# Linear attention and an eight-expert MoE on one core: q transposed before its feature map, k^T v and num in the same PSUM banks, loads and front order rewritten

## The chip, the cores and the metric

The kernel runs on one NeuronCore of a Trainium2 chip. A core has a matrix engine (TensorE, PE in the profile), a vector engine (VectorE, DVE), an activation engine (ScalarE, ACT), a general engine (GpSimd, POOL) and a synchronisation engine (SyncE, SP). Each of them takes its instructions strictly in the order in which they were written, and they wait for each other through semaphores. Matmul results land in PSUM, which has eight banks of 2 KB per partition; everything else lies in SBUF. Loads from memory are issued by POOL (which converts fp32 to fp16 on the way) or by SP, and run on 16 shared DMA engines. The metric is device time in microseconds of one execution; lower is better.

## The reference, cut to what matters

```python
def _attn_ref(q, k, v):                       # [8, 8, 576, 64] each
    def phi(x):
        return np.where(x > 0, x, np.exp(x) - 1.0) + 1.0
    q_p, k_p = (phi(q), phi(k))
    kv = np.einsum('bhsd,bhse->bhde', k_p, v)
    z = np.sum(k_p, axis=2)
    num = np.einsum('bhsd,bhde->bhse', q_p, kv)
    den = np.einsum('bhsd,bhd->bhs', q_p, z)[..., None] + 1e-06
    return num / den

def _moe_ref(x, w_gate, w1, w2):              # x [4608, 512], w1 [8, 512, 1024], w2 [8, 1024, 512]
    P = np.exp(logits - logits.max())         # logits = x @ w_gate, then 8 rounds of row and column scaling
    for e in range(E):
        out += P[:, e:e + 1] * (np.maximum(x @ w1[e], 0.0) @ w2[e])
```

The attention output, with its heads side by side, is the x of the MoE: 4608 tokens of 512 features. The feature map phi is computed as min(max(x + 1, 1), exp(x)).

## The kernel before

**Attention in units.** A unit is one batch and four heads; there are 16, in order. For each unit the kernel loads k, q and v (`att`, L385). k stays fp32; q is converted to fp16 by the load for all units but the first, and lies in three slots of the tile `hb`; v has three tiles `vv0` to `vv2`, with a third plane of ones that gives z beside kv. The load of k for unit 0 and of q for unit 0 are issued by SP, all others by POOL.

From k: ACT takes exp (`ek`, L417), DVE takes max(k + 1, 1) (`t`, L421) and the min of both (L425). PE multiplies this with v in 36 small matmuls (`kv_ps`, L446, 64 by 64 tiles), and ACT or DVE copies the 256 columns to SBUF (`kvz`, L359 or L361).

From q: ACT takes exp (`eq`, L477) and DVE takes max (`tq`, L480), both out of SBUF; DVE takes their min (L484); PE transposes the result in 36 steps into the two PSUM banks of the tile `att` (L469); DVE (for the last two units ACT) copies it to SBUF (`qpT`, L361 or L359).

Then, for each half c of the unit's tokens: PE computes den into the two banks of `att` (L504), ACT takes Ln of it (L516); after both halves ACT takes exp(-Ln) over both (`rden`, L521), which is 1/den; PE computes num (`num_ps`, L504), and DVE multiplies the two into `xT` (L531). `kv_ps` and `num_ps` are the same two banks, used in turn (the pool `p_kv` of one).

**MoE.** Tokens are taken in nine groups of 512. For expert 0, layer 1 (`hq`, L717) of a group follows as soon as its x is there, ACT or DVE applies the relu into `hb`, and layer 2 (`ye`, L1017) follows. For the later expert 0 groups and for experts 1 to 7, the two layers are computed with seven products of half blocks in place of eight (L832, L1133), which runs PE without a break from about 120 us to the end. The routing weights are computed on DVE with one small matmul per round (L589) meanwhile.

**Weights.** w1 of expert 0 comes in two halves of 512 columns, w2 of expert 0 in two halves of four row blocks; the first matmuls of layer 1 need the first half of w1, the others the second.

**What sets the order.** Every step is a task of a small planner (`_Plan`): it has an engine, a cost, dependences and the buffers it takes and frees. `run` goes through the tasks and writes out each one's instructions. For the first 2192 tasks, which cover the front up to about 190 us, the order is not chosen but read from a table of task numbers and engines, `_FRONT` (p PE, a ACT, d DVE, g POOL, s SP, m DMA, n none). So each engine's order in the front is fixed by this table, and an instruction that has to wait holds up everything behind it on its engine. A framework below adds the semaphore waits between engines when the instructions are written out. Until the first layer 1 matmuls, 46 dummy matmuls (`yw`, L621) keep PE running.

Of the kernel before, what the change touches and what calls it, by code (L numbers as in the profile page):

```python
# [141 lines left out]
1n 2p 3p 4p 5p 48s 49m 6p 7p 8p 0g 9p 10p 11p 12p 13p 14p 15p 16p 17p 18p 19p 20p 21p  # L142
22p 23p 54a 50s 51m 60n 61a 114g 115m 120a 24p 25p 55d 56d 62d 63d 26p 27p 52g 53m 64p 65d 57n 58p
121d 59a 28p 29p 75g 76m 77g 78m 82d 122d 30p 31p 66p 32p 33p 79g 80m 34p 116g 117m 35p 36p 37p 38p
39p 81a 87n 83d 89d 84n 67a 68p 40p 88a 90d 69a 70a 41p 85p 86d 91p 92d 42p 43p 73p 93p 44p 45p
74d 71p 126n 128d 104n 127a 118g 119m 94a 105g 106m 72d 46p 95p 96a 47p 129d 97a 123n 109n 124p 125d 130p 143g
144m 153n 579n 154a 131d 98p 99d 580p 141g 142m 581p 132p 133a 147a 100p 101d 582p 583p 584p 586p 588p 587a 148d 155d
585a 590p 107g 108m 145g 146m 134p 135a 589d 156d 149d 150n 592p 593a 594p 136a 170g 171m 180n 151p 152a 110g 111m 112g
113m 157p 158d 596p 139p 591a 140d 182d 159p 595a 160a 181a 598p 183d 168g 169m 172g 173m 137p 138d 161p 162a 597a 599a
197g 198m 195g 196m 175d 600p 602p 184p 185d 603p 610a 174a 176d 207n 616n 177n 601p 608a 163a 606p 607p 199g 200m 224g  # L150
225m 226g 227m 178p 179a 186p 187a 166p 167d 201a 208a 604p 236n 164p 209d 165d 202d 203d 210d 204n 188p 605p 617p 618a
619p 620d 621p 189a 190a 622a 211p 238d 253g 254m 212d 205p 230a 206a 228g 229m 251g 252m 280g 281m 102g 103m 282g 283m
231d 623p 625p 624d 626d 213p 193p 194d 237a 239d 232d 214a 627p 614a 628a 629p 215p 216a 217a 191p 192d 631p 649n 632a
233n 612d 240p 241d 234p 235a 255g 256m 637p 218p 242p 243a 635p 244p 630d 258d 257a 245a 219d 220p 259d 260n 284g 285m
263n 265d 221d 292n 334g 335m 293a 264a 287d 638p 636p 222p 643a 223a 650p 651a 652p 266d 645d 267p 246a 653a 311g 312m
309g 310m 307g 308m 261p 268d 314d 262d 286a 654p 656p 657a 655d 294d 319n 336g 337m 633p 269p 295d 249p 250d 658p 660p
659d 288d 321d 320a 270a 313a 639p 661a 247p 271p 272a 273a 315d 248d 662p 289n 340a 663a 296p 297d 290p 291d 322d 640p
361g 362m 338g 339m 274p 298p 275d 299a 365g 366m 634p 535d 300p 301a 276p 277d 367a 664p 536d 665d 316n 682n 317p 323p
318a 647a 302a 341d 363g 364m 392g 393m 390g 391m 542d 368d 324d 683p 684a 685p 342d 686a 346n 348d 347a 668p 278p 279a
373n 374a 543d 375d 687p 688a 303p 444g 445m 325p 326a 369d 537d 304d 689p 453s 376d 544d 349d 690a 641a 669p 305p 327p  # L160
328a 329a 691p 306d 343n 350p 692d 351d 344p 345a 446g 447m 454s 476g 477m 402n 396a 666p 330p 394g 395m 417g 418m 352p
353a 448g 449m 455s 404d 667p 397d 354p 403a 355a 331d 332p 474g 475m 483s 674a 356a 484s 370n 693p 333d 371p 372d 377p
378d 459n 405d 478g 479m 485s 419g 420m 695p 359p 379p 694a 538s 539m 360d 676d 398d 424d 461d 696a 380a 423a 460a 670p
671p 672p 357p 381p 382a 673p 697p 486g 358d 425d 462d 480a 406p 407d 698d 715n 399n 400p 429n 383a 680a 401a 481d 716p
717a 421g 422m 386p 408p 409a 545s 546m 431d 387d 718p 720p 719a 563d 564d 565d 566s 567m 430a 432d 410p 411a 384p 385d
678a 426n 482d 705p 547s 548m 706p 713a 721a 412a 433p 434d 427p 428d 549d 722p 435p 413p 724p 414d 436a 723a 550d 725d
437p 438a 439a 415p 416d 726p 463p 464a 556d 440p 557d 551d 540s 541m 490n 491a 552s 553m 492d 441d 451d 493d 558d 559s
560m 570g 554s 555m 487n 571n 572g 573m 574g 575m 701p 702p 388p 488p 450a 452d 389a 489a 494p 442p 443d 728p 709d 729d
456n 457p 495a 496p 497a 458d 703p 498p 499a 500a 501p 704p 727d 465p 466a 502d 711d 730p 731a 734p 467p 468a 469a 503p
504d 759d 760d 735p 742a 699p 472p 473d 700p 470p 471d 533n 755d 748d 981s 982m 983s 984m 749d 808d 750d 756d 561s 562m  # L170
707a 751s 752m 985s 986m 987s 988m 757d 758d 753s 754m 738p 739p 732p 763n 733p 534p 809d 810d 761d 811s 812m 813s 814m
989s 990m 991s 992m 505p 506a 740a 508d 507n 576n 577g 578m 764p 778p 765a 766p 767a 780p 781a 770p 771a 768p 769a 772p
736p 774p 993s 994m 779a 784p 785a 782p 783a 746a 773d 775d 509p 510d 786p 787d 788p 789d 776p 737p 973d 815n 777a 816p
817a 511d 790p 791a 818p 819a 822p 820p 744d 762d 821a 823a 830p 832p 833a 831a 824p 825d 794p 826p 866d 867d 827d 834p
836p 837a 838p 795p 840p 974d 868d 839d 869s 870m 828p 829a 512p 835a 841d 513d 802d 792p 793p 874p 875a 800a 876p 877a
1023s 1024m 1025s 1026m 568s 569m 1027s 1028m 842p 880p 798p 514d 924d 878p 843a 844d 881a 975d 925d 845d 926d 846d 515p 796p
799p 797p 804a 871s 872m 927s 928m 516d 929s 930m 873n 884p 882p 885d 883d 888p 848p 517d 879a 889a 894p 976d 886p 895a
849a 890p 891a 806a 898p 892p 893a 847d 899d 854p 887a 896p 518p 850p 851a 855a 519d 520d 897d 852p 900p 932p 901a 853a
858p 859d 856p 857d 946p 933a 938p 902d 903d 904d 939a 521p 934p 522d 860p 935a 861a 936p 942p 906p 948p 931n 937a 943d
947a 944p 952p 949a 940p 953a 523d 941d 908p 954p 955d 945a 950p 956p 907a 951a 995p 996a 909a 957d 524p 525d 526d 997p  # L180
958p 998a 1001p 1002a 912p 1003p 1004d 999p 1005p 1006d 959a 913a 916p 917d 910p 527p 905d 528d 529d 1007p 1009p 1011p 1000a 1010a
1012a 918p 1015p 1016a 1008a 1017p 1013p 1014a 1018d 1019p 919a 530p 531d 532d 712a 1020d 1037p 914p 1039p 1038a 613a 972n 1029s 1030m
1031s 1032m 1033s 1034m 1035s 1036m 1485n 1040a 977d 915d 960p 1021p 1043p 1119s 1120m 1121s 1122m 1123s 1124m 1486g 1487m 1488g 1489m 961p
968d 978d 1044a 1022a 1093d 962p 963p 969a 964p 864a 1045p 966p 1094d 979d 1041p 1095d 1046d 1042a 609a 1047p 611d 681a 965p 1048d
1049p 675d 1051p 1053p 648a 1052a 615d 980d 1054a 1050a 967p 1057p 1058a 1059p 1055p 1061p 1065p 1067p 1096d 971d 1062d 1060d 970d 1063p
1056a 1066a 1071p 1068a 911d 1073p 1069p 1097p 1099p 1100d 679d 1064a 1072a 1101d 1098a 1102p 1103a 1075p 1107p 1110p 1076d 1077p 1079p 1108d
1070a 743d 1111d 1109d 646a 1081p 1113p 1078a 1080a 1085p 1125s 1126m 1127s 1128m 1082a 1087p 1086a 1105a 714a 1104g 1106g 1129s 1130m 1083p
1074d 1089p 1133p 1135p 1084a 1114d 1112d 1088d 1115d 1116p 1090d 1091p 1131s 1132m 1241s 1242m 1243s 1244m 1245s 1246m 1490n 1491g 1492m 1134a
1139p 1136a 642a 1092a 1141p 1140a 1137p 1118d 1117d 1161d 1162d 1165p 1167p 1166a 1170p 1143p 1175p 1138a 644a 1163d 1164d 1169d 710d 1168d
1173a 1174g 1171a 1144d 1178p 1145p 1146a 1147p 1177d 1176d 708d 1172g 1148a 1149p 1150a 1181p 1153p 1179d 1142d 1154a 1155p 1151p 1157p 1183d  # L190
1180d 1182d 1158d 1187p 677a 1189p 1184p 1159p 1215d 1216d 1186d 747d 1185d 1217d 741d 1218d 1152a 1188a 1193p 801a 1190a 1195p 1191p 1219p
1221p 1194a 1222d 1196d 1223d 1192a 1220a 1224p 1227a 1228g 923a 1160a 1197p 1198d 1156d 1229p 1231d 1232p 1230d 1493d 865d 1233d 1199p 1200a
1201p 1202a 1203p 1204a 803a 1235p 1207p 1209p 1247s 1248m 1205p 1208a 1211p 1225a 1236d 1494d 1495d 1237d 1249s 1250m 1251s 1252m 1253s 1254m
1255p 1363s 1364m 1365s 1366m 1257p 1238p 1212d 1206a 1256a 1210d 1213p 1261p 1258a 1263p 1259p 1367s 1368m 1214a 807a 1240d 1234d 1239d 1287p
1262a 1288a 1283d 1289p 1292p 1284d 1285d 1293a 1291d 1290d 1286d 1265p 1297p 1300p 745d 1266d 1267p 1260a 1299d 1302d 1298d 1301d 1269p 1271p
1303p 1268a 1270a 1275p 1264d 1272a 1277p 1273p 1304d 1337d 1305d 1276a 1279p 1309p 1311p 1306p 1338d 1274a 1226g 1280d 1281p 1295a 1310a 863a
# [41 lines left out]
def kernel(  # L238
# [17 lines left out]
    P = 128  # L256
# [65 lines left out]
    p_ye = [S_.pool(1) for _ in range(4)]  # L322
    p_sw = S_.pool(8)

    def load_w(ten, nm, pl, pieces, e, prio, deps=(), shape=None):
        g = S_.grp(pl)
        ts_ = []

# [1020 lines left out]
```

## Time and profile before

| | |
|---|---|
| median of 3 runs | 951.25 us (950.62 to 951.71) |
| the profiled execution | 951.94 us |
| its span, first instruction to last | 950.1 us |
| PE busy | 939.9 us, 99% of the span |
| of this, the 46 dummy matmuls | 14.1 us |
| DVE, ACT, POOL busy | 765.3, 575.8, 144.3 us |
| granted TensorE clock | 1.00 in every stage |

The span is what the profiler saw of the program on the core; the execution's own time is 1.84 us more. A line of a timeline gives the start in us, the time to the end of the last of its instructions, the engine, the source line, the operation with its output and inputs, a count, and in brackets the idle time before it with what ended it. PE's matmuls overlap at their ends, so a block of four 512-column matmuls shows as 1.03 us and takes 0.865 of PE's time. Stages (answers by window) give each engine's busy time within that stretch.

### The profile page before, as it was taken

Reading aid. Unit: us, or ns where it says so; the run is one execution under the profiler, and the core shown is the slowest. Engines: PE = TensorE matmul, PEld = TensorE weight load, DVE = VectorE, ACT = ScalarE, POOL = GpSimd, SP = SyncE. Lnnn points to the kernel's source line nnn. Section 1 sums busy time; section 2 is a strip of 40 time slices with the busy share of each in tenths; the row PEclk is TensorE's granted clock in tenths of the full one; section 3 lists DMA queues with packets and bytes.
Section 4 is the critical chain, followed back from the end, with each engine's and each line's share of the span. In section 5 each row is a group of like instructions: output and inputs, shape, how many; then the busy total and the mean of one; then the engine's idle time right before and its main releaser. Section 6 shows DMA issues by size and latency. Waiting matters only on the chain.

```text
span 950.1 us, 19908 instructions
## 1 busy us (share of the span) xinstructions
PE 939.9 (99%) x7816; PEld 631.7 (66%) x7816; DVE 765.3 (81%) x1479; ACT 575.8 (61%) x1025; POOL 144.3 (15%) x204
## 2 busy tenths in 40 slices
PE   9999999999999999999999999999999999999997
PEld 4444478666676666766677666766667666776665
DVE  7699899879877888788887888878887888877776
ACT  6899856666655555555555555555555555555552
POOL 5433100011111111110011111111112111111110
PEclk9999999999999999999999999999999999999999
DMA  9989793452254222652236222652226422215544
GB/s 239 265 185 235 170 230 94 122 122 78 79 126 86 75 77 78 162 122 78 79 87 119 79 78 78 152 114 70 68 67 143 111 78 78 73 45 166 167 134 134
DMA packets 82042, 112.75 MB, mean 119 GB/s; under 512 B 7324, under 2 KB 46236, under 8 KB 81948
## 3 DMA queue, kind: packets, MB, share of 16 engines
q1 hardware_dynamic: 56876, 75.59, 26.0%
q0 software_dynamic: 24320, 34.78, 19.6%
q8 instruction: 61, 1.00, 0.4%
q10 hardware_dynamic: 752, 1.11, 0.3%
q14 instruction: 33, 0.27, 0.1%
HBM read 119.69 MB, written 17.69 MB: 145 GB/s over the span
## 4 chain that ended last, share of the span: by engine, by line
PE 94%; DMA 4%; ACT 1%; DVE 1%; POOL 0%; issue 0%
PE ye L1133 35%; PE hq L832 24%; PE R L832 12%; PE Zye L832 6%; PE Zye L1133 6%; PE ye L1017 5%; PE hq L717 3%; DMA w<-in_moe_w_dram 2%; DMA vv<-in_v_dram 2%; PE kv_ps L446 1%; PE att L504 0%; PE num_ps L504 0%; PE hq L1229 0%; DMA kin<-in_k_dram 0%; PE att L469 0%; PE R L1229 0%
## 5 line engine op out<-in xcount | busy, mean ns | idle before, releaser
L1164 DVE SCALAR_TENSOR_TENSOR acc<-ye,P_sb,acc 128x256 f32<-128x256 f32 x620 | 268.4, 479 | 126.9 <-PE ye L1133 126.2
L1133 PEld LDWEIGHTS <-S 128*128 128x128 f16 x1984 | 194.0, 98 | 46.6 <-DVE S L1104 0.2
L1133 PE MATMUL ye<-T,S 128*128 128x256 f16 x1488 | 192.8, 273 | 0.0
L1174 POOL TENSOR_TENSOR acc<-acc,st 128x256 f32<-128x256 f32 x124 | 88.1, 730 | 635.2 <-ACT st L1171 624.0
L832 PEld LDWEIGHTS <-W 128*128 128x128 f16 x1248 | 122.1, 98 | 86.6
L1133 PEld LDWEIGHTS <-hb 128*128 128x128 f16 x1536 | 150.3, 98 | 42.5 <-issue 1.3
L863 ACT ACTIVATE hb<-hq 128x512 f16<-128x512 f32 x134 | 80.2, 598 | 136.6 <-PE hq L832 130.2
L832 PE MATMUL R<-xs,W 128*128 128x512 f16 (+1 forms) x560 | 150.0, 358 | 0.0
L832 PE MATMUL hq<-xs,W 128*128 128x512 f16 (+1 forms) x560 | 150.0, 358 | 0.0
L832 PE MATMUL hq<-xs,w 128*128 128x512 f16 (+1 forms) x560 | 139.7, 358 | 0.0
L832 PEld LDWEIGHTS <-w 128*128 128x128 f16 x936 | 91.5, 98 | 59.8 <-issue 0.5
L860 ACT ACTIVATE hb<-Zye 128x512 f16<-128x512 f32 x134 | 80.1, 598 | 38.5 <-PE Zye L832 38.3
L1171 ACT ACTIVATE st<-Zye,P_sb 128x256 f32<-128x256 f32 x124 | 52.5, 471 | 77.2 <-PE Zye L1133 77.0
L866 DVE CUSTOM_DVE_ANT_0 hb<-hq,sx 128x512 f16<-128x512 f32 x126 | 86.6, 687 | 15.0 <-PE hq L832 14.9
L853 ACT COPY sx<-hq 128x512 f32<-128x512 f32 x126 | 73.6, 584 | 35.3 <-PE hq L832 35.3
L849 ACT COPY Zye<-hq 128x512 f32<-128x512 f32 x134 | 77.9, 581 | 22.6 <-PE hq L832 22.4
L866 DVE CUSTOM_DVE_ANT_0 hb<-R,sx 128x512 f16<-128x512 f32 x126 | 86.5, 687 | 4.9 <-ACT sx L853 3.8
L1104 DVE TENSOR_TENSOR S<-hb 128x1024 f16<-128x1024 f16 x124 | 85.0, 686 | 5.0 <-ACT hb L863 5.0
L832 PE MATMUL Zye<-xs,w 128*128 128x512 f16 (+1 forms) x280 | 75.0, 358 | 0.0
L857 ACT COPY sx<-R 128x512 f32<-128x512 f32 x126 | 74.4, 591 | 0.0
L1133 PE MATMUL ye<-w,hb 128*128 128x256 f16 x512 | 66.3, 273 | 0.6 <-DVE acc L1164 0.5
L1133 PE MATMUL Zye<-w,hb 128*128 128x256 f16 x512 | 66.3, 273 | 0.0
(119 smaller groups left out, 940.8 us busy)
## 6 DMA issues: line engine op xcount, KB each, us to landing
xs<-xd SPq DMA_DIRECT2D x196, 256.0 KB, 3.3
w<-in_moe_w_dram POOLq DMA_DIRECT2D x18, 512.0 KB, 7.7
kin<-in_k_dram POOLq DMA_DIRECT2D x15, 576.0 KB, 7.4
out_dram<-acc SPq DMA_DIRECT2D x61, 128.0 KB, 2.4
w<-in_moe_w_dram POOLq DMA_DIRECT2D x7, 1024.0 KB, 9.8
xs<-xd SPq DMA_DIRECT2D x49, 128.0 KB, 3.2
vv<-in_v_dram POOLq DMA_DIRECT2D x16, 288.0 KB, 7.2
hb<-in_q_dram POOLq DMA_DIRECT2D x15, 288.0 KB, 6.4
```

The source lines that it names most:

```text
L832: nc.tensor.matmul(dst_[:, p, :] if parts == 2 else dst_.rearrange("p a b -> p (a b)"), lhsT=lhs(p, c), rhs=blk[i](c), start=(first and p ...
L849: nc.scalar.copy(out=Zt[1], in_=gX["tile"])
L853: nc.scalar.copy(out=gs2["tile"], in_=gX["tile"])
L857: nc.scalar.copy(out=gs5["tile"], in_=gR["tile"])
L860: nc.scalar.activation(out=dst(0, 0), in_=Zt[1], func=AF.Relu)
L863: nc.scalar.activation(out=dst(1, 0), in_=gX["tile"], func=AF.Relu)
L866: nc.vector._custom_dve(TENSOR_ADD_SAT, out=out_, in0=ps, in1=sb, s0=3.0e38, s1=0.0)
L1104: nc.vector.tensor_tensor(out=Sx[:, i], in0=a0, in1=a1, op=op)
L1133: nc.tensor.matmul(bank(g_)[:, s, :], lhsT=lhs(s, kk), rhs=rhs(kk), start=(new and s == 0 and kk == 0), stop=(kk == 3), skip_group_check=True)
L1164: nc.vector.scalar_tensor_tensor(out=dst(), in0=bank(g_)[:, s, :], scalar=P_sb[:, gg, e:e + 1], in1=dst(), op0=ALU.mult, op1=ALU.add)
L1171: nc.scalar.mul(out=gst["tile"], in_=bank(g_)[:, s, :], mul=P_sb[:, gg, e:e + 1])
L1174: nc.gpsimd.tensor_tensor(out=dst(), in0=dst(), in1=gst["tile"], op=ALU.add)
```

## The change

1. **q is transposed as loaded** (units 1 to 15). PE transposes the raw fp16 q into PSUM; ACT's exp and DVE's max then both read the transposed q from PSUM and write SBUF, and DVE's min gives `qpT` there. The copy out of PSUM is gone, and so is the tile `tq` but for unit 0, which goes as before. Unit 1 uses the banks of `ye0` and `ye1` in place of `att`, with exp and max in halves.
2. **k^T v beside num.** One tile `kvn` of two banks is taken once. num uses its columns 0 to 287, kv its columns 384 to 511; the planner has a pool for each, where one served both.
3. **Loads.** w1 of expert 0 comes in three pieces, of 256, 256 and 512 columns; all loads are made to follow the first of their queue, and their order on POOL is new: v0, k1, q1, v1, w1 (two pieces), q2, k2, v2, w1 (last), k3, q3, v3, w2 (two pieces), and so on, where it was k1, v0, k2, q1, v1, q2, v2, w1, q3, k3, w1, v3, q4, w2, w2.
4. **exp(-Ln) in halves** for the first two units.
5. **38 dummy matmuls** in place of 46, new costs in the planner, and a **new table** `_FRONT`.

```diff
-    p_kv = S_.pool(1)
+    p_kv, p_num = S_.pool(1), S_.pool(1)
+    kvn = kvps.tile([P, 2, 512], FP32, tag="kv", name="kvn")
...
-            gkv["tile"] = kvps.tile([P, 2, 512], FP32, tag="kv", name="kv_ps")
+            gkv["tile"] = kvn[:, :, 384:384 + 2 * D]
...
-            return load_w(moe_w1, "w1", p_w1, [[((slice(None), slice(None), slice(512 * i, 512 * i + 512)),
-                                                 512 * i, [[F, P], [P * F, NDT], [1, 512]])] for i in range(2)], e, shape=[P, NDT, F], **kw)
+            return load_w(moe_w1, "w1", p_w1, [[((slice(None), slice(None), slice(a, a + n)),
+                                                 a, [[F, P], [P * F, NDT], [1, n]])] for a, n in ((0, 256), (256, 256), (512, 512))],
+                          e, shape=[P, NDT, F], costs=(0.0013 * 1024, 0.0013 * 1024, 2.65), **kw)
...
-                        nc.tensor.transpose(qps()[half(r), hh, j, :], gtq["tile"][half(hh), j, r, :],
+                        nc.tensor.transpose(qin(hh)[half(r), j, :],
+                                            gtq["tile"][half(hh), j, r, :] if n == 0 else gin["q"]["tile"][half(hh), r, j, :],
                                             ident[half(hh), half(hh)])
...
+            t1 = fadd(("pe", 0.29), f_qt, deps=[tin["q"], t_id[0]], acq=ga, use=[gin["q"]], prio=pr, cfg=1)
+            t0 = fadd(("none", 0.0), f_qa, deps=[t1], acq=[geq], prio=pr)
+            ta = fadd(("none", 0.0), f_gq, deps=[t1], acq=[gq], prio=pr)
+            te2 = []
+            for hs in range(2 if n == 1 else 1):
+                def f_qe(_, hs=hs):
+                    o, i = qio(geq["tile"], hs)
+                    nc.scalar.activation(out=o, in_=i, func=AF.Exp)
+
+                def f_qm(_, hs=hs):
+                    o, i = qio(gq["tile"], hs)
+                    nc.vector.tensor_scalar(out=o, in0=i, scalar1=1.0, scalar2=1.0, op0=ALU.add, op1=ALU.max)
+                us = [ga[hs]] if n == 1 else ga
+                te2.append(fadd(("act", 0.65 if n == 1 else 1.16), f_qe, deps=[t0], use=[*us, geq], prio=pr))
+                te2.append(fadd(("dve", 0.44 if n == 1 else 0.76 if b < NR else 1.36), f_qm, deps=[ta], use=[*us, gq], prio=pr))
+
+            def f_qp(_):
+                nc.vector.tensor_tensor(out=gq["tile"], in0=gq["tile"], in1=geq["tile"].rearrange("p r j d -> p r (j d)"), op=ALU.min)
+            tq = fadd(("dve", 0.76), f_qp, deps=te2, use=[geq, gq], prio=pr)
...
-            gn = S_.grp(p_kv)
+            gn = S_.grp(p_num)
...
-                gn["tile"] = kvps.tile([P, 2, 512], FP32, tag="kv", name="num_ps")
+                gn["tile"] = kvn[:, :, 0:CH]
...
-    for i in range(46):
-        twa = add(("pe", 0.43 if i < 9 else 0.215), f_warm, deps=[twa], use=[gyw], prio=900.0, after=1.2 + 0.25 * i)
+    for i in range(38):
+        twa = add(("pe", 0.43 if i < 14 else 0.215), f_warm, deps=[twa], use=[gyw], prio=900.0, after=1.2 + 0.25 * i)
...
-            t1 = add(("pe", 0.2175 * (c1 - c0)), f_hq, deps=[tw1[0 if g == 0 and f < 4 else 1], prev_hq[0]] + xd_[0:c1 if g == 0 else None],
+            t1 = add(("pe", 0.2175 * (c1 - c0)), f_hq, deps=[tw1[f // 2 if g == 0 and f < 4 else -1], prev_hq[0]] + xd_[0:c1 if g == 0 else None],
```

Here n is the unit, b its batch, `qin` and `qio` give the PSUM view of the transposed q (for unit 1 one bank per half), and `p r j d` are partition, head pair, token block and feature.

More of the change, by code (lines that the diff above doesn't have):

```diff
@@ L323, with load_w @@
     p_sw = S_.pool(8)
-    def load_w(ten, nm, pl, pieces, e, prio, deps=(), shape=None):
+    def load_w(ten, nm, pl, pieces, e, prio, deps=(), shape=None, costs=None):
         g = S_.grp(pl)
@@ L445, in f_kv @@
                     for r in range(2):
-                        nc.tensor.matmul(gkv["tile"][half(r), hh, 0:2 * D].rearrange("p (z d) -> p z d", z=2),
+                        nc.tensor.matmul(gkv["tile"][half(r), hh, :].rearrange("p (z d) -> p z d", z=2),
                                          lhsT=gt["tile"][half(hh), j, r, :], rhs=gin["v"]["tile"][half(hh), r:r + 2, j, :],
@@ L456, in f_z, with qin @@
         def f_z(e):
-            copy(e, gz["tile"], gkv["tile"][:, :, 0:2 * D].rearrange("p h (z d) -> p h z d", z=2))
+            copy(e, gz["tile"], gkv["tile"].rearrange("p h (z d) -> p h z d", z=2))
         tz = [fadd({"dve": 0.43, "act": 0.37}, f_z, deps=[tkv], use=[gkv, gz], prio=pr)]
         gq, geq = S_.grp(p_qpT), S_.grp(p_eq)
-        ga = [S_.grp(p_att), S_.grp(p_att)]
+        ga = [S_.grp(p_ye[0]), S_.grp(p_ye[1])] if n == 1 else [S_.grp(p_att), S_.grp(p_att)]
         def qps():
             return at2.bitcast(FP16)[:, :, 0:S].rearrange("p h (j w) -> p h j w", w=PW)
+        def qin(hh):
+            if n == 1:
+                return ga[hh]["tile"].bitcast(FP16)[:, 0:S].rearrange("p (j w) -> p j w", w=PW)
+            return qps()[:, hh]
         def f_qt(_):
+            for hh in range(2 if n == 1 else 0):
+                ga[hh]["tile"] = yps.tile([P, 512], FP32, tag=f"ye{hh}", name=f"ye{hh}")
             for j in range(NJ):
@@ L473, in f_qa @@
             geq["tile"] = fp.tile([P, 2, NJ, D], FP16, tag="ek", name="eq", bufs=3)
-            gtq["tile"] = fp.tile([P, NJ, 2, D], FP16, tag="tq", name="tq")
-        def f_qe(_):
-            nc.scalar.activation(out=geq["tile"], in_=gin["q"]["tile"], func=AF.Exp)
-        def f_qm(_):
-            nc.vector.tensor_scalar(out=gtq["tile"].rearrange("p j r d -> p r j d"), in0=gin["q"]["tile"], scalar1=1.0, scalar2=1.0, op0=ALU.add, op1=ALU.max)
-        def f_qp(_):
-            tv = gtq["tile"].rearrange("p j r d -> p r j d")
-            nc.vector.tensor_tensor(out=tv, in0=tv, in1=geq["tile"], op=ALU.min)
@@ L486, in f_qc, with f_gq, qio @@
-        def f_qc(e):
+            if n == 0:
+                gtq["tile"] = fp.tile([P, NJ, 2, D], FP16, tag="tq", name="tq", bufs=1)
+        def f_gq(_):
             gq["tile"] = fp.tile([P, 2, S], FP16, tag="qpT", name="qpT")
+        def qio(t, hs):
+            dst = t.rearrange("p r j d -> p r (j d)") if len(t.shape) == 4 else t
+            if n == 1:
+                return dst[:, hs], qin(hs).rearrange("p j w -> p (j w)")
             if b >= NR:
-                copy(e, gq["tile"].rearrange("p h (w j) -> p h w j", j=NJ), qps().rearrange("p h j w -> p h w j"))
-            else:
-                copy(e, gq["tile"], at2.bitcast(FP16)[:, :, 0:S])
@@ L492, in att @@
[L492 to L498 removed]
+                return dst.rearrange("p h (w j) -> p h w j", j=NJ), qps().rearrange("p h j w -> p h w j")
@@ L499, in att @@
+        tqs = [tq]
         grd = S_.grp(p_rden)
@@ L521, in f_ex, with f_exh @@
             nc.scalar.activation(out=grd["tile"], in_=grd["tile"], func=AF.Exp, scale=-1.0)
-        te_ = fadd(("act", 1.18), f_ex, deps=tl, use=[grd], prio=pr)
+        te_ = []
         for c in range(2):
-            gn = S_.grp(p_kv)
+            def f_exh(_, c=c):
+                nc.scalar.activation(out=grd["tile"][:, c], in_=grd["tile"][:, c], func=AF.Exp, scale=-1.0)
+            if n < 2:
+                te_.append(fadd(("act", 0.62), f_exh, deps=[tl[c]], use=[grd], prio=pr))
+            elif c == 0:
+                te_ = [fadd(("act", 1.18), f_ex, deps=tl, use=[grd], prio=pr)] * 2
+        for c in range(2):
+            gn = S_.grp(p_num)
             def f_num(_, c=c, gn=gn):
-                gn["tile"] = kvps.tile([P, 2, 512], FP32, tag="kv", name="num_ps")
+                gn["tile"] = kvn[:, :, 0:CH]
                 heads(gn["tile"], c, 0)
@@ L636 @@
     gsw = S_.grp(p_sw)
-    ti = add(("pool", 0.8), f_wg, acq=[gsw], use=[gsw], prio=-96.5, after=1.75)
+    ti = add(("pool", 0.8), f_wg, acq=[gsw], use=[gsw], prio=-96.5, after=1.75, deps=[first_ld["pool"]])
     wg_done.append(add(("dma", 0.3), lambda _: None, deps=[ti], use=[gsw], prio=-96.5, lat=2.15))
```

233 lines of the change are left out of this document (125 added, 108 removed).

## The prediction

> **What bounds the kernel now.** First the page's busy times and slices, then the table of 10 us stages, then PE's timeline where a stage is not full, last one unit of attention followed over three engines.
>
> ```profile
> PE 939.9 (99%) x7816; PEld 631.7 (66%) x7816; DVE 765.3 (81%) x1479; ACT 575.8 (61%) x1025; POOL 144.3 (15%) x204
> DMA  9989793452254222652236222652226422215544
> ```
>
> TensorE is the bound; DMA is full only in the first 100 us.
>
> ```profile
> 10.00:20.00 10.00, 9.40 (x260) 4.80 (x253) 8.51 (x14) 7.86 (x10) 5.79 (x8) 1.00 1.18 197
> 20.00:30.00 10.00, 9.28 (x149) 4.12 (x138) 6.55 (x11) 8.32 (x13) 4.32 (x6) 1.00 1.20 235
> 30.00:40.00 10.00, 8.84 (x120) 3.95 (x118) 5.11 (x8) 7.66 (x12) 2.87 (x4) 1.00 1.16 282
> 90.00:100.00 10.00, 9.03 (x178) 4.20 (x173) 9.50 (x17) 9.41 (x15) 1.50 (x2) 1.00 0.86 205
> 100.00:110.00 10.00, 9.68 (x240) 5.20 (x233) 9.19 (x19) 8.25 (x11) 0.00 (x0) 1.00 0.56 162
> ```
>
> The columns are stage, length, and busy us of PE, PEld, DVE, ACT, POOL. Every other stage from 40 to 190 is full, and from 200 to the end PE lacks 5.1 us, mostly the tail. So the end moves by what PE gains or loses before about 125 us, where attention ends.
>
> ```profile
> 20.60 1.04 PE L717 MATMUL hq<-xT,w 128*128 128x512 f16 x4
> 25.66 1.90 PE L717 MATMUL hq<-xT,w 128*128 128x512 f16 x8 [0.56 <-DMA w<-in_moe_w_dram]
> 34.09 3.61 PE L1017 MATMUL ye<-w,hb 128*128 128x512 f16 x16 [0.68 <-DMA w<-in_moe_w_dram]
> 38.82 0.32 PE L504 MATMUL att<-qpT,kvz 64*64 64x288 f16 x4 [0.48 <-ACT kvz L359]
> 99.75 0.47 PE L446 MATMUL kv_ps<-vv,t 64*64 64x128 f16 x18 [0.97 <-DMA vv<-in_v_dram]
> 108.29 0.48 PE L469 MATMUL att<-ident,tq 64*64 64x64 f16 x36 [0.32 <-ACT P_sb L552]
> ```
>
> The first useful layer-1 matmul is at 20.60. Twice PE then waits for expert 0's weights; after 34.09 it loses only 0.48 + 0.97 + 0.32 = 1.77 us.
>
> ```profile
> 40.06 0.45 DVE L480 TENSOR_SCALAR tq<-hb 128x1152 f16<-128x1152 f16 x1
> 40.88 1.15 ACT L477 ACTIVATE eq<-hb 128x1152 f16<-128x1152 f16 x1
> 44.12 0.48 PE L469 MATMUL att<-ident,tq 64*64 64x64 f16 x36
> 44.73 0.76 DVE L361 COPY qpT<-att 128x1152 f16<-128x1152 f16 x1
> 46.87 0.32 PE L504 MATMUL att<-qpT,kvz 64*64 64x288 f16 x4
> ```
>
> One unit's q: max and exp read SBUF and need not wait for each other, min follows, and only then PE transposes; the banks "att" have one reader, the 0.76 us copy.
>
> **Method.** I laid the changed kernel's built order out in time, instruction by instruction: each instruction starts at the later of its engine's previous end and the end of what it waits for (plus 0.2 after PE, 0.05 after ACT or DVE), with durations from the rows above and their like (min 0.75, x product 0.76, Ln 0.73, exp 1.16, kvz copy 0.37 on ACT, ye or hq block of four 0.865, kv 0.53, PE turn between 64- and 128-row tiles 0.13). The old order so laid out puts the first hq at 20.2 (trace 20.6), the wait at 38.4 at 0.62 (trace 0.48) and the end at 949.1 (span 950.1).
>
> **Loads (a gain).** POOL's old queue stood until 6.12 for the first k buffer; the new one issues v0, k1, q1, v1, both 256-column pieces of w1 and q2 before the load that needs it. v0 takes k1's place and lands at about 8.2 (k1: 1.46 + 6.7). On SP nothing moves. The gate copy on POOL now stands ahead of v14 and the last four q: the layout has the last v land 0.7 before its kv, so 0; at worst the 0.97 of the old 99.75 comes back. Ahead of the second w2 piece stands one q load less: -1.45 (w1's first half landed at 20.2, the q behind it at 21.65). The 256-column rows make 512-byte packets, which no load here has: by bytes alone the two cost what the one did (+0), by packets alone twice 2.5 instead of 2.5 (+2.5). Single cast packets took 98 ns at 1024 bytes, 107 at 1152 and 172 at 2048; their line gives 61 at 512, so +0.65, which I take. With 0.3 for the earlier start, w2's second piece lands at about 33.0 instead of 34.1: **-1.1**. The first hq comes out at 16.8, 3.8 earlier, but that is not the gain: PE runs into w2. Eight warm matmuls fewer cost nothing, since the rest only fill PE before 16.8. For the first two units exp is cut in halves, not seen here: 0.58 (half of 1.16) to 0.73 (Ln of 576), I take 0.66; hidden behind w2.
>
> **Old waits.** The 1.77 us after 34.09 belonged to the old order; I count them as gone: **-1.8** (bounds 0 and -1.8).
>
> **Engine work.** Fifteen copies go (13 x 0.76 DVE, 2 x 1.1 ACT). max, 0.45 on fp16 in SBUF, now reads fp16 in PSUM. Not in this trace; the nearest row is the copy of the same 1152 elements from the same bank, 0.76, which I take; bounds 0.45, and 1.45 if it runs at the fp32 PSUM pace (0.76 for 576). exp from PSUM stays 1.16 (ACT's copy of the bank took 1.10). Six kvz copies go from DVE to ACT, 0.37 each. All of this lies beside PE; alone it moves nothing.
>
> **New waits (loss).** The built order of the changed kernel (line numbers of its own) shows what each instruction waits for. Two engines that read or write one PSUM tile's bank now wait for each other, even in different columns:
>
> ```
> L531 Activation eq_940<-att_78 128x1152 [waits DVE_49,PE_49]
> L535 TensorScalarPtr qpT_941<-att_78 128x1152 [waits Activation_49]
> L362 TensorCopy kvz0_103<-kvn_108 128x256 [waits DVE_49]
> ```
>
> Here max (L535) waits for the exp of the same q in 11 of the 14 units 2 to 15, in units 7, 9 and 15 exp waits for max; the copy of kv (L362) waits for an x product reading num in other columns, x products wait for kv copies, and kv's matmuls wait for x products. The planner's tasks name none of these as dependences, so its fixed order puts nothing there to cover them. From transposes to den: 0.2 + 1.16 + 0.05 + 0.76 + 0.75 = 2.9 us, where side by side it would be 2.1. And DVE is a queue: while max waits, x products behind it wait, and PE's second num waits for them.
>
> Unit 5: transposes end 46.5; exp 46.7 to 47.9; max 47.9 to 48.65; x of unit 4 behind it 48.6 to 49.35; num, which needs its bank, at 49.4. PE has only a 0.87 block, to 48.17, and the turn: 1.1 idle.
> Unit 13: transposes end 104.1; the kv copy must also wait for num in its bank, exp 105.8 to 107.0, max to 107.8, two queued DVE steps, min 109.1 to 109.8, den 109.8. PE is done at 108.0: 1.7 idle.
> Unit 15: kv waits for unit 14's x, behind max: 1.4 idle at 122.3; then the kvz copy behind exp and that x: 1.4 at 127.2.
>
> All waits after the second w2 piece, in order from 38 us: 0.71, 1.11, 0.77, 0.50, 0.87, 0.44, 0.35, 0.57, 0.50, 0.56, 1.09, 0.13, 0.51, 1.66, 0.24, 0.50, 1.39, 1.42: **+13.3**. Before w2 they cost nothing, as w2 is later (den of unit 3 is ready at 30.5, w2's first piece at 30.4). No filler can come forward: the order is a fixed list. In the same layout the waits of "att" alone come to 10.9, those of the kv and num banks alone to 4.7; they overlap.
>
> **Sum.** -1.1 - 1.8 + 13.3 = +10.4 on a span of 950.1 gives 960.5; with the 1.84 us around it (951.94 - 950.1) 962.3. The profiled execution stood 0.7 above the median of 951.25, so the median becomes **961.7**.
>
> **The rule weighed.** The Trainium skill, "PSUM — Partial Sum Buffer", section "PSUM bank collisions raise a hardware error", says that no two engines may be in one bank at a time, reads against reads included, and that they must be kept apart by bank. By that rule the waits cannot be dropped and the sum stays 961.7; without them it would be 948.4. No run here shows a collision. On max's price, "VectorE: DVE Perf Modes", section "Why PSUM operands drop a tier", caps an operand in PSUM one step below what SBUF allows; that speaks for 0.76 against 0.45 (959.0 by 0.45).
>
> **Rivals.**
> 1. Faster: the bank waits fall under PE's blocks, because Ln, exp and kv copies land otherwise than laid out. Then -1.1 - 1.8 = -2.9: 948.4. For it: old PE had 100% in 40 to 90 with DVE at 85 to 100%. Against: a block is 0.87 and the chain 2.9, and DVE's queue passes each delay on. It decides where the 18 waits sum to under 2.9 us.
> 2. max from PSUM costs 1.45: each of 14 chains is 0.69 longer; laid out so, the end comes 7.9 later: 969.6. For it: fp32 from PSUM runs at that pace; against: the fp16 copy's 0.76.
> 3. Half of the waits are absorbed (max at 0.45, PE turns shorter): +6.6 - 2.9 = +3.7: 955.
> 4. The 512-byte packets cost the full 2.5: w2 at 34.9, +1.9 on the sum: 963.6.
>
> **Chances.** Forecast 0.66 with rival 4 inside it (957 to 966), rival 2 0.12, rival 3 0.14, rival 1 0.05, within 0.2% 0.03. 0.2% (1.9 us) is about what a measurement can tell. Faster 0.05, same 0.03, slower 0.92. The range leaves out rival 1, half of rival 2 and some of rival 3: 956 to 969.
>
> **What will show it.** After: first hq near 16.8; w2's second piece near 33; from 38 to 128 us a dozen or more PE waits of 0.4 to 1.7, put down to DVE xT, DVE qpT and ACT kvz; DVE's max starting where ACT's eq of the same unit ends; max 0.76 long; from 200 us on no difference but the offset. Wrong if the PE stages from 40 to 130 stay full, or max and exp of one unit overlap.

## The result: 1.5% slower, and the profile after

The changed kernel takes 965.65 us (median of 4 runs, 965.26 to 966.16), the kernel before 951.10 (4 runs, 950.62 to 951.71). The ratio is 1.0153, with a 95% interval of 1.0135 to 1.0171. The profiled execution took 965.41 us with a span of 963.6, 13.5 more than the 950.1 of before.

The page of the changed kernel, the lines that answer to those of before:

```profile
PE 938.9 (97%) x7808; PEld 632.7 (66%) x7808; DVE 765.1 (79%) x1469; ACT 574.4 (60%) x1024; POOL 145.3 (15%) x205
PE   8888889999999999999999999999999999999997
DMA  9978586435226322542226422442226522215544
```

PE is busy as long as before, but for 97% of the span and not 99%: the time is added as idle PE, and the six slices with an 8 say that it lies in the first 145 us.

The stages of the changed kernel (stage, length, then busy us of PE, PEld, DVE, ACT and POOL, the granted clock, DMA's share, GB/s):

```profile
10.00:20.00 10.00, 9.36 (x169) 4.39 (x168) 7.45 (x12) 9.43 (x14) 5.61 (x7) 1.00 1.26 234
20.00:30.00 10.00, 7.16 (x144) 3.52 (x143) 6.92 (x11) 7.52 (x11) 3.67 (x5) 1.00 1.21 239
30.00:40.00 10.00, 8.82 (x119) 4.30 (x119) 5.97 (x9) 7.12 (x9) 3.58 (x5) 1.00 1.19 292
...
90.00:100.00 10.00, 9.45 (x129) 3.98 (x127) 7.31 (x14) 7.88 (x10) 4.12 (x6) 1.00 1.00 168
100.00:110.00 10.00, 7.51 (x119) 3.62 (x119) 7.64 (x13) 6.29 (x9) 0.00 (x0) 1.00 0.72 188
...
120.00:130.00 10.00, 7.42 (x116) 3.52 (x116) 7.11 (x12) 7.21 (x11) 2.11 (x4) 1.00 0.36 108
...
140.00:150.00 10.00, 8.87 (x67) 6.20 (x65) 7.50 (x18) 5.42 (x10) 0.00 (x0) 1.00 0.90 235
```

No stage from 20 to 130 is full. DVE, which stood at 9.19 us in 100 to 110 before, has 7.64 there now, and ACT 6.29: no other engine has become the bound there. All of them wait for each other. The two long stages together, of before and then of the changed kernel:

```profile
38.00:130.00 92.00, 90.24 (x1479) 45.34 (x1469) 81.99 (x146) 78.69 (x112) 23.18 (x32) 1.00 0.93 210
130.00:200.00 70.00, 69.98 (x527) 50.98 (x525) 62.55 (x134) 44.67 (x84) 2.13 (x3) 1.00 0.44 123
```

```profile
38.00:130.00 92.00, 79.96 (x1383) 38.60 (x1369) 71.76 (x115) 71.12 (x97) 21.79 (x31) 1.00 0.74 167
130.00:200.00 70.00, 68.33 (x553) 50.85 (x552) 63.84 (x139) 42.63 (x80) 1.74 (x3) 1.00 0.68 166
```

So PE loses 90.24 - 79.96 = 10.28 us from 38 to 130, and 69.98 - 68.33 = 1.65 from 130 to 200. Up to 38 us it gains 0.60: 32.25 us busy less 11.10 of dummy matmuls, against 34.67 less 14.12. Behind 200 us it loses 0.15. That is 11.5 of the 13.5; the other 2.0 are a longer busy time for the same 7770 matmuls (927.8 against 925.8 without the dummies), which the stages can't place.

A second reading can. I weighed each matmul by its pitch in a full stage (0.2165 us for 512 columns, 0.1087 for 256, and so on), summed what PE had done by a given time, and looked up when the kernel before had done as much. The changed kernel's lag by equal work is then (some 0.3 us exact, minus means ahead):

| time in the changed kernel, us | 30 | 38 | 60 | 80 | 100 | 120 | 130 | 146 | 152 | 200 |
|---|---|---|---|---|---|---|---|---|---|---|
| lag, us | -0.6 | -0.9 | 1.5 | 4.0 | 6.0 | 8.6 | 11.1 | 11.1 | 13.1 | 13.3 |

The lag grows steadily through attention by 12.0 us, stands still, jumps by 2.0 between 146 and 152 us, and then nothing more happens. PE's waits in the changed kernel (waiting and releasing line, us, times, longest):

```profile
PE att L549 <- DVE qpT L541: 4.2, 4, 1.6
PE kvn L453 <- DVE xT L583: 2.4, 4, 1.3
PE kvn L549 <- DVE xT L583: 2.2, 4, 1.1
PE att L549 <- DVE qpT L535: 1.4, 2, 0.9
...
PE att L549 <- ACT kvz L362: 1.3, 1, 1.3
PE kvn L549 <- ACT kvz L362: 1.2, 2, 0.6
PE R L641 <- DVE gs L636: 1.1, 1, 1.1
```

In the kernel before no wait of PE for another engine's step in attention came to more than 0.5. What these steps had waited for themselves stands in the view of max's line (durations in ns, shortest, median and longest, then the idle time ahead of it):

```profile
L535 DVE TENSOR_SCALAR qpT<-att x14: 757/758/1357, 20.4 to 121.9; 128x1152 f16<-128x1152 f16 x14
...
its engine sat idle before it (us, times) until:
  ACT eq L531: 11.6, 11
```

11 times of 14 DVE stood idle until ACT's exp of the same q (L531) had ended, 11.6 us in all. One unit, picked from the timelines of the three engines:

```profile
46.21 0.48 PE L483 MATMUL att<-ident,hb 64*64 64x64 f16 x36
46.81 1.11 ACT L531 ACTIVATE eq<-att 128x1152 f16<-128x1152 f16 x1
47.25 1.04 PE L1069 MATMUL ye<-w,hb 128*128 128x512 f16 x4
47.95 0.76 DVE L535 TENSOR_SCALAR qpT<-att 128x1152 f16<-128x1152 f16 x1 [1.71 <-ACT eq L531]
48.63 0.75 DVE L583 TENSOR_TENSOR xT<-kvn,rden 128x576 f16<-128x576 f32 x1
49.29 0.75 DVE L541 TENSOR_TENSOR qpT<-qpT,eq 128x1152 f16<-128x1152 f16 x1
49.43 0.32 PE L549 MATMUL kvn<-qpT,kvz 64*64 64x288 f16 x4 [1.15 <-DVE xT L583]
```

exp ends at 47.92, max starts at 47.95, with 1.71 us of DVE idle before it; the x product (L583), which had nothing to do with this q, stands behind max in DVE's queue, and PE's num waits 1.15 us for the bank that x frees.

### The profile page after: what moved, and what is told of

Its sections match the earlier page's. It is cut to its first block, busy times and chain, and to the rows that moved or that the text cites. A ratio compares the mean times of both kernels' runs of the same rounds, so it can differ in the third digit from the quotient of the medians.

```text
span 963.6 us, 19841 instructions
## 1 busy us (share of the span) xinstructions
PE 938.9 (97%) x7808; PEld 632.7 (66%) x7808; DVE 765.1 (79%) x1469; ACT 574.4 (60%) x1024; POOL 145.3 (15%) x205
## 4 chain that ended last, share of the span: by engine, by line
PE 87%; DVE 5%; DMA 4%; ACT 2%; issue 1%; POOL 0%; POOLq 0%; DVEq 0%
PE ye L1185 35%; PE hq L884 23%; PE R L884 12%; PE Zye L1185 6%; PE Zye L884 6%; DMA w<-in_moe_w_dram 3%; PE ye L1069 3%; PE hq L769 1%; ACT eq L531 1%; DMA kin<-in_k_dram 1%; DVE xT L583 1%; DVE qpT L535 1%; DMA xd<-acc 1%; DVE t L432 0%; DVE qpT L541 0%
```

## The experiments

**Theory A**: two engines that use one PSUM tile wait for each other; the fixed order was made without these waits, and that is the loss in attention. **Rival B**: the loss lies in the new operations and their longer chain (transposes, exp, max, min, den through one pair of banks), which no order covers. The jump at 146 us is a question of its own. Times are given against runs of the kernel before on the same chip (951.9 to 952.2 us).

### The two load orders

DVE's and PE's timeline at the jump, in the changed kernel:

```profile
145.24 0.69 DVE L1111 TENSOR_TENSOR W<-w 128x1024 f16<-128x1024 f16 x1 [2.29 <-DMA w<-in_moe_w_dram]
...
148.16 0.45 DVE L636 TENSOR_REDUCE gs<-wt 128x8 f32<-128x288 f32 x1
...
148.67 0.39 PE L641 MATMUL R<-gs,ones_t 128*128 128x8 f32 x2 [1.13 <-DVE gs L636]
```

A sum over expert 1's weights stands at the head of DVE's queue until its load lands; behind it stand the six small steps of a routing round, and PE's matmul of that round waits 1.13 us, and a product after it 0.41 for the DVE step behind those. In the kernel before POOL loads w1 of expert 1 ahead of its w2; the new table has it behind (570 and 572 issue w1, 575 issues w2).

```diff
-500d 730p 731p 738a 733p 501p 502d 531n 746d 747d 748d 740a 734p 736p 735p 532p 568g 574n 569n 575g 576m 570g 571m 762p
-763a 753d 754d 755d 572g 573m 749s 750m 756d 742a 806d 979s 980m 503p 504a 506d 505n 766p 767a 807d 776p 777a 981s 982m
+500d 730p 731p 738a 733p 501p 502d 531n 746d 747d 748d 740a 734p 736p 735p 532p 568g 569n 574n 570g 571m 572g 573m 575g 576m 762p
+763a 753d 754d 755d 749s 750m 756d 742a 806d 979s 980m 503p 504a 506d 505n 766p 767a 807d 776p 777a 981s 982m
```

> The changed kernel, only that POOL issues the two loads of expert 1's w1 ahead of its w2 (as the kernel before does) and not behind it. Theory A: after attention the lag grows by 2.0 us between 146 and 152 us, because DVE's sum of w1's halves waits 2.29 us for that load and the routing steps queued behind it come late, so PE waits 1.13 and 0.41 us; with w1 first these waits go and the median falls by about 2.0, to 963.6 us. Rival: the load is late whatever its place, since it is issued at 128 us only; then the wait and the time stay (965.6).

Measured: 963.88 us, a ratio of 1.0118 (1.0097 to 1.0139). The profile has no PE wait between 130 and 200 us any more, and 69.99 us of PE there. The lag by equal work is 10.6 at 140 and 10.4 at 200, without a jump. The two halves of w1 now land 6.2 us after their issue (median), where it was 14.4 behind w2. As theory A said for this place.

POOL's gate copy was the second. It waits for v of unit 15, and the new table put it ahead of six loads, four of q and two of v (the expectation below says seven, and the prediction names five of them):

```diff
-484g 446g 447m 690a 665p 692d 390g 391m 376d 352p 693p 444g 445m 353a 547d 417g 418m 354a 451s 452s 453s 481s 355p 377p
+446g 447m 690a 665p 692d 390g 391m 376d 352p 693p 444g 445m 353a 547d 417g 418m 354a 451s 452s 453s 481s 355p 377p
...
-403a 382p 678a 483s 549d 404d 383d 714p 405d 422d 419g 420m 668p 669p 399a 384p 406p 407a 449d 423d 676d 385d 713n 715a
+403a 382p 678a 483s 549d 404d 383d 714p 405d 422d 419g 420m 484g 668p 669p 399a 384p 406p 407a 449d 423d 676d 385d 713n 715a
```

> The changed kernel with w1 of expert 1 loaded ahead of its w2, and besides with POOL's gate copy (which waits for v of unit 15) put behind the last loads of q and v, where the changed kernel has it ahead of seven of them. Theory A: PE's wait for a q load near 96 us (0.56 in the changed kernel, 0.73 with w1 first) goes as well, so about 0.6 less than with w1 first alone: 1.1% above the kernel before. Rival: the q load is late for its own buffer or the queue of transfers, and the wait stays (1.2% above).

Measured: 962.97 us, 1.0116 (1.0101 to 1.0132), the same as with w1 first alone. The mechanism was right and the gain was not. The two lines of the kernel with w1 first, and then the one that answers to them with the gate copy moved too:

```profile
95.82 0.48 PE L483 MATMUL att<-ident,hb 64*64 64x64 f16 x36 [0.73 <-DMA hb<-in_q_dram]
...
99.96 0.32 PE L549 MATMUL kvn<-qpT,kvz 64*64 64x288 f16 x4 [0.34 <-ACT kvz L362]
```

```profile
102.09 0.32 PE L549 MATMUL kvn<-qpT,kvz 64*64 64x288 f16 x4 [1.14 <-ACT kvz L362]
```

The 0.73 for q is gone, and the next wait, num for the copy of kv, is 1.14 in place of 0.34 (together 1.07 and 1.14). ACT's copy doesn't come earlier when PE does; the wait is only taken elsewhere. (In this profile the granted clock was 0.96 up to 38 us, so its span of 962.9 is not compared.)

### The waits taken away

For max, its source is changed. The comparison gives ones: max(q + 1, 1) is left out, and phi is min(1, exp(q)).

```diff
+                    if n > 1:
+                        x = ident[:, None, :].to_broadcast([P, 9, P])
+                        nc.vector.tensor_tensor(out=gq["tile"].rearrange("p h s -> p (h s)").rearrange("p (a w) -> p a w", a=9), in0=x, in1=x, op=ALU.is_ge)
+                        return
                     nc.vector.tensor_scalar(out=o, in0=i, scalar1=1.0, scalar2=1.0, op0=ALU.add, op1=ALU.max)
```

> The changed kernel, only that for units 2 to 15 DVE's max does not read the transposed q in PSUM, but compares one constant SBUF tile with itself over as many fp16 elements (left out: max of q; the tensor-tensor form is taken so that it lasts as long, 0.75 us). So max no longer has to wait for exp, nor exp for max, all else stays in its order. Theory A (the two engines' waits for each other's use of one PSUM tile make the loss): laid out in time, the waits from 38 to 128 us fall from 13.3 to about 4.4, the median to about 956.7. Rival B (the loss lies in the new order, longer chains and turns of PE, and not in these waits): no more than 2 us off, 963.6 or above.

Measured: 958.51 us, 1.0063 (1.0044 to 1.0083), where the changed kernel has 1.0153; the replacement took 0.75 us, as it should. PE has 85.99 us in 38 to 130 where it had 79.96. Theory A's 956.7 was 0.6% above the 951.1 it was worked out against, so it is met in the ratio; rival B's 963.6 is not. What is left in this kernel's timeline of PE:

```profile
91.82 0.48 PE L483 MATMUL att<-ident,hb 64*64 64x64 f16 x36 [2.23 <-DMA hb<-in_q_dram]
...
114.79 0.70 PE L453 MATMUL kvn<-vv,t 64*64 64x128 f16 x36 [1.31 <-DVE xT L587]
...
119.70 0.32 PE L553 MATMUL att<-qpT,kvz 64*64 64x288 f16 x4 [1.27 <-ACT kvz L362]
...
141.80 0.39 PE L645 MATMUL R<-gs,ones_t 128*128 128x8 f32 x2 [1.49 <-DVE gs L640]
```

The waits for max and min are gone, the two of unit 15 at kv's bank (1.31 and 1.27) are as they were, and the two loads cost more than in the changed kernel (2.23 and 1.49 against 0.56 and 1.13): PE gets there 6.2 and 7.2 us earlier, but what it waits for comes only 4.5 and 6.9 us earlier.

For the banks of kv and num, the x product leaves num out.

```diff
-                                        in0=gn["tile"][:, :, 0:CH], in1=grd["tile"][:, c], op=ALU.mult)
+                                        in0=grd["tile"][:, c], in1=grd["tile"][:, c], op=ALU.mult)
```

> The changed kernel, only that DVE's x product multiplies the reciprocal in SBUF with itself and not num in PSUM (left out: the product with num). So neither kv's matmuls nor kv's copies meet x in the shared banks; num loses its own wait for x too. Theory A: laid out in time, 5.0 us less, a median of about 960.7; the waits that are left are those for max and min. Rival B: within 1 us of the changed kernel (964.6 or above).

Measured: 961.62 us, 1.0099 (1.0073 to 1.0125); 960.7 against 951.1 would be 1.0101. PE has 83.94 us in 38 to 130. Both edits in one kernel:

> Both edits together: max from a constant in SBUF, x without num (left out: max of q and the product with num). Theory A: of the waits behind 38 us one of 0.6 is left, 13.0 us less, and with the late load of expert 1 still there a median of about 952.7. Rival B: 963 or above. Rival C (the waits overlap so that either edit alone already gives all of it): 956 to 957, as with max alone.

Measured: 958.36 us, 1.0060 (1.0036 to 1.0083): theory A's 952.7 fails, and rival C's number is met, but not by what C says. The waits did add up: PE has 89.14 us in 38 to 130, 3.2 more than with max alone. What took the gain are the loads, and in the profiled execution the granted clock behind them as well:

```profile
90.47 0.48 PE L483 MATMUL att<-ident,hb 64*64 64x64 f16 x36 [2.38 <-DMA hb<-in_q_dram]
...
140.59 0.59 PE L645 MATMUL R<-gs,ones_t 128*128 128x8 f32 x2 [3.67 <-DVE gs L640]
```

```profile
90.00:95.00 5.00, 4.53 (x85) 2.17 (x86) 3.25 (x5) 1.92 (x4) 1.43 (x2) 0.66 1.13 176
...
140.00:145.00 5.00, 4.41 (x13) 2.06 (x14) 4.79 (x14) 0.00 (x0) 0.00 (x0) 0.50 0.63 167
```

Around each of the two waits the granted clock fell, to a mean of 0.66 from 90 to 95 us and to 0.50 from 140 to 145; the eight matmuls after the second wait took 3.57 us, where eight such take 1.89 elsewhere. By the stages of 5 us from 90 to 150 this cost up to 5 us, an estimate: about as much as theory A missed by. The other three executions had a mean clock of 0.995 to 0.998, so how much of the median is the wait and how much the clock behind it is not known. The test of that reading is the same kernel with both load orders mended:

> Max from a constant and x without num (left out: max of q and the product with num), and both load orders mended. Theory A: with the waits between the engines gone, only the two load orders still cost (2.38 for q, 3.67 in the routing); with them mended the layout gives 947.3 against 949.1 for the kernel before, so 0.2% below it (0.997 to 1.001). Rival: what is left of the loss is in the front or in PE's turns; then 0.4% above or more.

Measured: 949.79 us, 0.9979 (0.9969 to 0.9989). The expectation of 0.2% below is met. PE has 90.36 us in 38 to 130 and 69.98 in 130 to 200, and one wait above 0.5 behind 38 us (1.17 for a q load at 88.90). The clock is 1.00 in the stages of this profile, so a part of the 8.6 us between the two kernels can be the clock. With the waits and the two load orders gone, nothing of the loss is left: it was not in the front, nor in PE's turns, nor in the operations' durations.

### The same operations in another order

Nothing is left out here. The table for the first 720 entries (attention and what runs beside it) was planned anew, each operation starting when its engine is free and all that it needs is there, with durations from the traces, and with one thing added: an operation on a PSUM tile also waits for the last one of every other engine on that tile. The two mended load orders are kept. 26 copies and relus changed between ACT and DVE, two more of them on DVE in all.

```diff
-1n 100n 577n 107n 40s 41m 42s 43m 2p 3p 0g 4p 44g 45m 5p 6p 68g 69m 7p 8p 70g 71m 9p 72g
-73m 10p 47d 46a 11p 101g 102m 12p 48d 13p 103g 104m 52n 53a 14p 54d 15p 114g 115m 16p 55d 17p 112g 113m
+40s 1n 41m 42s 43m 0g 2p 44g 45m 3p 68g 69m 70g 100n 4p 5p 6p 71m 47d 72g 73m 101g 7p 8p
+102m 9p 103g 104m 52n 114g 46a 53a 10p 115m 112g 113m 11p 12p 48d 54d 55d 116g 117m 13p 14p 15p 49n 56p
...
```

> The changed kernel's own instructions, all of them, with a new table of the order for the front: planned with the waits between engines on one PSUM tile counted as dependences, loads in the changed kernel's order but for the two mends (w1 of expert 1 first, gate copy last). Theory A: the loss is not in the operations but in an order that does not know these waits; laid out in time it ends at 947.1 against 949.1 for the kernel before and 960.3 for the changed one, so 0.2% below the kernel before (0.997 to 1.002). Rival: the chain transposes, exp, max, min, den through one pair of banks is too long to be covered in any order; then 1.006 or above.

Measured: 949.69 us (11 runs, 949.49 to 950.47), 0.9979 (0.9971 to 0.9988): 0.2% faster than the kernel before, where the changed one is 1.5% slower. Rival B falls: the chain through the two banks can be covered. The stages, and what max met:

```profile
38.00:130.00 92.00, 90.45 (x1457) 46.49 (x1455) 83.29 (x144) 77.83 (x109) 22.44 (x31) 1.00 0.92 205
130.00:200.00 70.00, 69.98 (x526) 50.87 (x524) 62.11 (x134) 45.95 (x87) 3.72 (x5) 1.00 0.49 131
```

```profile
L535 DVE TENSOR_SCALAR qpT<-att x14: 748/758/1359, 18.2 to 110.1; 128x1152 f16<-128x1152 f16 x14
...
its engine sat idle before it (us, times) until:
...
  ACT eq L531: 1.8, 2
```

DVE waits for exp before max twice, 1.8 us, where it was 11 times and 11.6 us. The wait between the engines is still in the program; other work lies in it. The same unit's steps show how:

```profile
43.44 1.11 ACT L531 ACTIVATE eq<-att 128x1152 f16<-128x1152 f16 x1
43.21 0.75 DVE L432 TENSOR_TENSOR t<-t,ek 128x1152 f16<-128x1152 f16 x1
43.87 0.75 DVE L583 TENSOR_TENSOR xT<-kvn,rden 128x576 f16<-128x576 f32 x1
44.58 0.76 DVE L535 TENSOR_SCALAR qpT<-att 128x1152 f16<-128x1152 f16 x1
```

While exp reads the banks, DVE does k's min and the x product that had stood behind max, and max starts when exp has ended, with no idle before it.

Two controls. In the first every operation keeps its engine, so that the order alone differs:

> As the replanned kernel, but every operation stays on the engine on which the changed kernel has it (the replanned one had moved 26 copies and relus between ACT and DVE), so that the order alone differs. Theory A (the order's ignorance of the waits is the loss): laid out in time 950.0 against 949.1 for the kernel before and 960.3 for the changed one: 0.1% above the kernel before (0.999 to 1.005). Rival (the choice of engines did it): 1.008 or above.

Measured: 952.33 us (10 runs), 1.0004 (0.9995 to 1.0013). With the order alone the loss is gone. The last 0.25% to the replanned kernel may be the freedom of engines, a luckier plan, or the clock: in this profile PE waits 1.80 and 1.33 us for loads ahead of 7.98 and 10.85 us, and

```profile
10.00:15.00 5.00, 4.15 (x88) 2.02 (x89) 2.64 (x6) 3.20 (x6) 2.59 (x4) 0.50 1.34 202
```

the granted clock is 0.50 from 10 to 15 us. All ten executions have a mean clock of 0.995 to 0.998, those of the replanned kernel 0.999 to 1.000. These two runs don't separate the three. In the second the plan is made as freely as in the replanned kernel, but does not count the waits:

> A control: the same planning, with the same start, load order and free choice of engines as the replanned kernel, but without counting the waits between engines on one PSUM tile. To itself that plan looks as good as the replanned one (146.2 against 146.6 us at the same place in the work). Theory A: with the waits that the framework then adds, the layout ends at 958.9, 1.0% above the kernel before (1.007 to 1.013). Rival (any fresh plan is better than the changed kernel's table): 1.002 or below.

Measured: 963.24 us, 1.0123 (1.0106 to 1.0140). A plan that looked as good to itself is as slow as the changed kernel with its loads mended, and with the same kind of waits:

```profile
48.10 0.70 PE L453 MATMUL kvn<-vv,t 64*64 64x128 f16 x36 [1.02 <-DVE xT L583]
...
70.95 0.32 PE L549 MATMUL att<-qpT,kvz 64*64 64x288 f16 x4 [1.34 <-ACT eq L531]
...
102.88 0.32 PE L549 MATMUL kvn<-qpT,kvz 64*64 64x288 f16 x4 [1.45 <-DVE kvz L364]
...
126.28 0.32 PE L549 MATMUL att<-qpT,kvz 64*64 64x288 f16 x4 [1.05 <-DVE qpT L541]
```

That settles the theory: the same operations and the same effort of planning, with and without knowledge of the waits, differ by 1.4%. (One plan of each kind was run.)

### w1 in two pieces again

```diff
-                                                 a, [[F, P], [P * F, NDT], [1, n]])] for a, n in ((0, 256), (256, 256), (512, 512))],
+                                                 a, [[F, P], [P * F, NDT], [1, n]])] if n else [] for a, n in ((0, 512), (0, 0), (512, 512))],
```

> The changed kernel, only that the first two pieces of expert 0's w1 (256 columns each) are one load of 512 columns again. The layout priced the packets of 512 bytes at 0.65 us for the pair: the last half of w1 and w2 then land 0.65 earlier, and the end comes about 0.6 to 1.0 earlier (0.1% below the changed kernel). If the packets cost nothing, no difference; if they cost twice their bytes, 2 us less. In the trace: the landing of w1's last half, and PE's wait for it of 0.87 us at 23.2.

Measured: 964.47 us, 1.0137 (1.0119 to 1.0155); against the changed kernel's 1.0153 (1.0135 to 1.0171) that decides nothing. In the trace the wait of 0.87 for w1's last half is gone, as the layout had it; but it is gone too in the profile with w1 of expert 1 first, where the pieces are as in the changed kernel, so the pieces need not be the reason. The first hq comes at 16.82 in place of 16.41, and den of unit 3 waits 1.53 us at 30.17 in place of 1.43 at 30.62. The lag by equal work at 38 us is -0.9 in both. The packets can be read in the changed kernel's trace: 1024 of 512 bytes, a median of 60 ns each, where those of 1024 bytes took 98. So the price was estimated well (61 ns), but it was not what counts there: PE's next stop is set by DVE's chain of unit 3, not by a load.

## Why the prediction was right, and where it was off

It gave 961.7 (956 to 969) and slower at 0.92; measured were 965.65, +14.4 us on the 951.25 of before where +10.4 was forecast. By its steps:

- **New waits, +13.3, with the old ones of -1.8 gone: +11.5.** By equal work the lag grew by 12.0 from 38 to 130 us. The trace lists 18 waits there, one of them for a q load, mostly in the layout's order, but they sum to 12.0 and not to 13.3; less the old 1.8 that is 10.3. The other 1.7 or so of the lag are PE busy longer over the same matmuls, for which the sum has no term by name, so the total agrees better than its parts. The single waits came out as laid out: 1.15 for num of unit 5 (1.1), 1.60 for den of unit 13 (1.7), 1.31 and 1.27 in unit 15 (1.4 and 1.4). That they come from the engines' waits on one tile is shown by taking these away and by the two plans.
- **max from PSUM, 0.76.** It measured 0.758 in 12 of 14 units; rival 2 (1.45) falls. That it is slower than the 0.45 out of SBUF agrees with the Trainium skill, "VectorE: DVE Perf Modes", section "Why PSUM operands drop a tier". Units 14 and 15 took 1.36, where I had priced all at 0.76, although the planner's cost in the change names 1.36 for them: they read and write a permuted layout. exp of q took 1.13 (1.16), the halves of exp(-Ln) 0.68 (0.66).
- **Loads, -1.1.** The size is about right (0.6 to 0.9 ahead at 38 us), the reason is not, so the agreement is luck. PE never waits for w2: it is held by den of unit 3 (1.43 us, at 30.62, for DVE's min L541) and goes from there through w2's first 28 matmuls without a stop. I had put that wait at 30.5, w2's first piece at 30.4 and its second at 33.0, and taken the last for the bound. Rival 4 (the packets of 512 bytes at their full price, w2 later by 1.9) falls with this: they took 60 ns, and w2 was not the bound. (Packets of 512 bytes did stand in the trace before, on SP's queue; on POOL's there were none.)
- **The gate copy, 0.** There was a wait of 0.56 for a q load at 96.33, within the bound of 0.97 I had set. In the place where the layout has a wait of 1.09, the trace has this one and then 0.52 for the kv copy; with the gate copy moved it has 1.14 for the kv copy alone. So moving it gained nothing, and the 0 was right in effect.
- **"From 200 us on no difference", and no term between 130 and 200.** The first holds to 0.15 us; the second is the step that failed. The loads of expert 1 were not in the sum: a swap of two entries behind attention, in a load order that I had followed up to w2 of expert 0 only. It cost 2.0 us by equal work, the largest miss. "DMA is full only in the first 100 us" was a misreading on the same path: the row shown has a 9 in its sixth slice, 119 to 142 us, where these loads run.
- **From the profile to the median.** I took the median as 0.7 below the profiled execution, as it was before; after, the profiled execution lay 0.24 below its median, which makes 0.9 us of the miss.

Together, over the forecast: 2.0 (expert 1) + 0.5 (attention) + 0.9 (profile to median) + 0.3 (front) = 3.7 of the 3.95. Rival 3 (half of the waits absorbed, 955) falls, as the lag grew by 12.0 and not by half of that. Rival 1 falls as a forecast, but its number was close to what the operations can do: 948.4 was named for the case that the waits are covered, and the replanned kernel has 949.69.

Not settled: why POOL issues expert 1's loads late in some profiles. With w2 first, POOL stood idle 1.51 us ahead of the first of these loads in four profiles and 0.35 in a fifth (w1 in two pieces), which then had no wait in the routing; with w1 first it was 0.35 in all six profiles. What the 1.51 is was not found. With w2 first and POOL in time, w1 landed 13.0 us after its issue and DVE waited 0.23 for it; with w1 first it landed after 6.2. So the order decides how early w1 lands, but that it costs PE time is shown only where POOL is late, and no run has w1 first with POOL late. And which of the changes makes the 0.2% of the replanned kernel was not tried part by part; by equal work it is 1.7 us ahead of the kernel before at 38 us already and 2.2 at 200, which points to the loads and the front.

## What to carry to other kernels

An order that is written out by hand or read from a table is only as good as its list of dependences: list for every engine what the framework will make it wait for, shared PSUM tiles above all, reads against reads too, before moving a second reader into PSUM. When such waits cost, the remedy is not to shorten the operations but to put other work of the waiting engine in between; the same operations here went from 1.5% slower to 0.2% faster. And when a wait is taken away, look at once for the load, copy or queue entry that is late next: three times in these runs it took a part or all of the gain.

## What the runs showed that was not expected

- The transposed fp16 q of the last two units, read and written in permuted order, takes DVE 1.36 us, against 0.76 for the same 1152 elements in plain order out of the same banks.
- The granted TensorE clock fell to a half for 3.4 or 6.8 us in four of the profiles (the end of the span left aside), in a kernel whose stages otherwise show 1.00: with both waits taken away (around 92 and 142 us), with x without num (around 146), with both load orders mended (30 to 35) and with the order alone changed (9 to 16). A pause of PE stands at or just before each of these places: 2.38 and 3.67 us, 2.25, 1.43, and 1.80 followed by 1.33. A pause does not always bring it: after 2.23 us with max alone, 2.73 in the plan without the waits and 1.60 in the changed kernel the stages stay at 1.00. What decides is not shown, but a wait can cost more than its length: by the stages up to 5 us in the kernel with both waits taken away, an estimate.
